# Booked arrivals of q and k stacks, row maxima on GpSimd's DMA queue, and a reordered start of the output projection in an attention and GLU kernel

## The chip, the cores and the metric

The kernel runs on one core of a Trainium2 chip. The metric is the device time of one execution in microseconds. Engines are named as in the profile: PE is TensorE, DVE is VectorE, ACT is ScalarE, POOL is GpSimd, SP is SyncE, which here issues nearly all DMAs.

## The reference

```
x: (1, 2048, 576)   wqkv: (576, 1728)   wo: (576, 576)
w_gate, w_up: (576, 4608)   w_down: (4608, 576)          all float32

xn = layernorm(x)
q, k, v = split(xn @ wqkv) into 32 heads of 18 columns
p  = softmax(q k^T / sqrt(18))           # 2048 x 2048 per head
s  = (p v) @ wo
b  = ((xn @ w_gate) * (xn @ w_up)) @ w_down
out = x + s * silu(b)
```

## The kernel before, in words

**Number format.** Products are made of float32r parts: a value is split into a high part (an ACT copy that rounds) and a low part (a subtraction on DVE or POOL), and high x high, high x low and low x high are summed. For q and k the parts lie above each other in the partitions: a *stack* has three times 18 rows. `ring` and `pair0`, `pair1` are tiles of 128 partitions; rows 0 to 53 serve the a items of a head, rows 64 to 119 the b items. `load_pair(r, h)` fetches a whole stack (three DMAs, 0.44 MB), `load_ring(r, h, k)` half of one (three DMAs, 0.22 MB), both from the scratch `sqk` in HBM by SP's queue.

**Stages.** First layernorm, q, k and v; then the main loop (`order`), which holds attention and the GLU at once; then the output projection (line 1156 to the end), which multiplies by `wo`, applies silu and adds x.

**Attention in the main loop.** A head has 64 *a items* and 64 *b items*. An a item (`a_item`) is a product q k^T of 128 queries by 512 keys and DVE's maximum of each row. After the last a item of a head, `max_fold` and `max_rows` fold the maxima, split them, transpose them into the tile `mt`, and write them with four DMAs of 4 KB as two more rows (R and R + 1) of the q stack that the b items use; the last head writes them to both row halves. A *b item* (`b_item`) is a product k q^T with these rows in it, and ACT's exponential into a `pt` tile. A *visit* multiplies up to seven blocks of four pt tiles by v (`pv_group`, L625); where it ends a head, `finish` divides on DVE and stores the result to `sot` with four DMAs on SP.

**The GLU in the main loop.** The work is cut in 72 units: 4 chunks c of 512 rows of x by 18 slices q of the hidden width. Two *streams* use the two halves of PE's rows (0 to 63 and 64 to 127) side by side: stream 0 makes the up products, stream 1 the gate products (L658, 27 for each of a unit's two parts n), and both make the down products of the unit before (L700). `gate_end` multiplies gate and up on DVE, splits on ACT and POOL (hs, L674) and fetches the next weights `wgu`; `turn_round` copies hs across the two halves as `hx`. At the end of a chunk the next x columns come in 18 loads (`x_block`).

**The planner.** The order of all these instructions is decided while the program is written, by a loop in `order` that keeps a clock for each stream (`clk`), for DVE, ACT and POOL (`free`), and one for the DMA engines (`queue`). `moved(start, size)` books a transfer: the queue moves on by size / 0.24 (MB and us) and the transfer counts as there 2.0 us later. `can_go` holds a stream's next product until the booked wgu, hx, wd or x is there. If a stream is held, an a or b item may be taken in its place. Items otherwise go by goals (`a_goal`, `b_goal`): b items follow `N + LEAD` = 88 places behind a items, and `b_ready` asks for the maxima to be there (`rows_done`, DVE's end plus 6.0 us).

Wanted stacks wait in the list `stacks`. They are sent at gate ends, up to two at a time, and this is booked; those left over are sent by `feed` at items 20, 48 and 52 of a head, and this is not booked. No a or b item asks when its stack arrives.

```
f(*a)
moved(fin + 1.4, 0.44 if f is load_pair else 0.22)      # at a gate end
...
want[0](*want[1])                                        # in feed
```

The loads of `wo` (`wo_load`, 1.47 MB) are not booked either, nor SP's wait at `finish`.

**The start of the projection.** After the last visit, `prefetch` puts `high` (ACT, L805) and `low` (DVE, L810) of the first three row blocks of the attention result, columns 0 to 511, in the list `later`; `small` takes from it while the last down products are planned. Behind the loop come five `w_split` (wo's high parts on ACT, L817, low parts on POOL, L818), and then `chores_done` empties the list.

Engines run their own instructions in program order. SP and POOL issue DMAs in that order too, and an issue that waits holds those behind it.

Of the kernel before, what the change touches and what calls it, by code (L numbers as in the profile page):

```python
# [40 lines left out]
def kernel(  # L41
# [98 lines left out]
    def chores_done():  # L140
        while chores or later:
            chore()
# [421 lines left out]
    with ExitStack() as mid:  # L564
# [27 lines left out]
        def max_rows(h):  # L592
            m = ms.pop(h)
            mm = mp.tile([128, 2, NT], FR, name="mm", bufs=1)
            mt = mp.tile([128, 32], FT, name="mt", bufs=1)
            nc.vector.tensor_scalar(mm[:, 0, :], m, -1.0, None, op0=OP.mult)
            nc.vector.scalar_tensor_tensor(mm[:, 1, :], m, -1.0, mm[:, 0, :].bitcast(FT),
                                           op0=OP.mult, op1=OP.subtract)
            nc.vector.transpose(mt, mm.rearrange("p a t -> p (a t)").bitcast(FT))
            for r in (64, 0) if h == H - 1 else (64,):  # L600
                q = ring if r == 0 else pairs[h % 2]
                for g in range(4):
                    rows = q[r + R:r + R + 2, :].rearrange("j (t g i) -> j g t i", g=4, i=32)[:, g].bitcast(FT)
                    nc.sync.dma_start(rows, mt[32 * g:32 * g + 32, :])

        pt, PARTS = {}, 29

# [172 lines left out]
        def prefetch(now):  # L780
            mid.close()
            ep = fin["ep"] = ctx.enter_context(tc.tile_pool(name="end", bufs=1, reuse_waits="tile"))
            loads.extend((fetch, (t,), 0.59) for t in range(4))
            quiet[0] = max(clk) + 2.0
            for k in range(3):
                later.extend([(high, (k, 0)), (low, (k, 0))])

        def begin():
            lo.extend(stk.tile([128, S], FR, name=f"o{k}", tag=tag) for k, tag in enumerate(("pair0", "pair1", "ring")))
# [41 lines left out]
        def stream(r):  # L831

            for u in range(len(units) + 1):
                for n in (2 * u, 2 * u + 1):
                    if u == len(units):
                        break
                    c, q = units[u]
                    box = []
                    for k in range(len(TERMS)):
                        def work(n=n, k=k, box=box, c=c, q=q):  # L840
                            if k == 0:
                                box.append(gu_start(r, n))
                            gu_op(r, n, box[0], k)
                            if q == NF2 - 1 and n % 2 and k % 3 == 2 and c < NCH - 1:
                                x_block(c + 1, k // 3, (64 * r,))
                                there["x", c + 1, k // 3, r] = moved(clk[r] + 0.5, 0.262)
                            if k == len(TERMS) - 1:
                                (gate_end if r else up_end)(n, box[0])
                                if r and n == 2 * len(units) - 1:
                                    wo_load()  # L850
                        end = (("DVE", 0.60) if r else ("ACT", 0.50)) if k == len(TERMS) - 1 else None
                        yield LONG, k == 0, work, end, ("g", n, k)
                for s in range(4):
                    if not u:
                        break
                    box = []
                    for k in range(len(DTERMS)):
                        def work(s=s, k=k, box=box, u=u - 1):
                            if k == 0:
                                box.append(down_start(r, u))  # L860
                            down_op(r, u, s, box[0], k)
                            if k == len(DTERMS) - 1:
                                down_end(r, u, s, box[0])
                        end = ("DVE", 0.365) if k == len(DTERMS) - 1 else None
                        yield SHORT, k == 0, work, end, ("d", u - 1, 12 * s + k)
# [16 lines left out]
        def next_free(tag):  # L882
            if tag == "g":
                return min(banks["g"])
            return banks[tag][turn[tag] % len(banks[tag])]

        def engine(eng, start, taken):
            free[eng] = max(free[eng], start) + taken
            return free[eng] + TAIL[eng]
# [26 lines left out]
            return a_goal(i) if i < TOTAL else a_goal(TOTAL) + LAST * (i - TOTAL)  # L916


        def feed(r, h, i):

            if i == 0:
                if h:
                    stacks.append((load_ring, (r, h, 1)))
                if h + 1 < H and (r or h):
                    stacks.append((load_pair, (r, h + 1)))
            if i == 32 and h + 1 < H:
                stacks.append((load_ring, (r, h + 1, 0)))
            for at, want in ((20, (load_ring, (r, h, 1))), (48, (load_pair, (r, h + 1))), (52, (load_ring, (r, h + 1, 0)))):
                if i == at and want in stacks:
                    stacks.remove(want)  # L930
                    want[0](*want[1])

        def a_next(r=0):
            nonlocal na
# [11 lines left out]

        def b_ready(r=1):
            h = nb // N
            return nb < TOTAL and rows_done.get(h, 1e9) <= clk[r] and len(due) * 4 + nb % 4 + 1 <= PARTS

        def b_next(r=1):
            nonlocal nb
# [46 lines left out]
        def visit(now):  # L999

            now = max(now, *clk)
            many = 0
            now += 0.095
            if due:
                now = max(now, next_free("g") - EARLY + 0.03)
            for h, t, at in due:
                if at > now + 0.5 * many + 0.3 or many == size(due[0]):
                    break
                now += 0.859
                many += 1  # L1010
            now -= 0.859 * many
            for h in sorted({h for h, _, _ in due[:many]}):
                ts = [t for g, t, _ in due[:many] if g == h]
                now = max(now, next_free("g") - EARLY + 0.03) + 0.859 * len(ts)
                k = banks["g"].index(next_free("g"))
                pv_group(h, ts, k)
                end = engine("DVE", now + 0.25, 0.60) if ts[0] else engine("ACT", max(now + 0.25, shown[0]), 0.495)
                banks["g"][k] = end + EARLY
                if ts[-1] == NT - 1:
                    finish(h)  # L1020
                    engine("DVE", end, 0.60)
                    engine("DVE", 0.0, 0.85)
                    shown[0] = engine("DVE", 0.0, 0.60)
            del due[:many]
            clk[0] = clk[1] = issued[0] = now + 0.13
            fresh[:] = True, True
# [40 lines left out]
        def order():  # L1067
# [5 lines left out]
            while any(heads) or na < TOTAL or nb < TOTAL or due:  # L1073
# [18 lines left out]
                lean = PULL * (gone[0] - gone[1] - SKEW) * (1 if r else -1)  # L1092

                if r == 0 and (na < TOTAL or nb < TOTAL - N) or r == 1 and nb == 0 and na < N:
                    at, goal, score, can = next_free("a"), a_goal(na) + lean, a_next, na < TOTAL and na < nb + N + MOST
                    can = can and not late(goal, r)
                else:
                    at, goal, score, can = next_free("b"), b_goal(nb) + lean, b_next, b_ready(r)
# [9 lines left out]
                elif op is not None:  # L1108
# [8 lines left out]
                    if end:  # L1117
# [9 lines left out]
                        elif r == 0:  # L1127
                            upped[n] = done
                        else:
                            gated[n] = done  # L1130
                            fin = engine("ACT", done + 0.05, 0.535)
                            fin = engine("POOL", fin + 0.05, 1.29)
                            loaded[n] = moved(done - 0.4, 1.18) if (n // 2 + 1) % NF2 else 0.0
                            if n // 2 == len(units) - 1:
                                there["h", n // 2] = moved(fin, 0.524)
                            elif n == 1:
                                there["h", 0] = moved(fin, 1.05)
                            for _ in range(2):
                                hot = n + 2 >= 2 * NF2 and n % (2 * NF2) in (34, 35, 0) and n + 2 < 2 * len(units)
                                for want in stacks:  # L1140
                                    if hot and (want[0] is load_pair or n % (2 * NF2) == 2 * NF2 - 1):
                                        continue
                                    stacks.remove(want)
                                    f, a = want
                                    f(*a)
                                    moved(fin + 1.4, 0.44 if f is load_pair else 0.22)
                                    break
                    heads[r] = next(feeds[r], None)
                else:
# [11 lines left out]
        f(*a)  # L1161
    for k in range(5):
        w_split(k)
    chores_done()
    for t in range(12, NT):
        def end_silu(e, t=t):
# [100 lines left out]
```

## Time and profile before

| | us |
|---|---|
| median of 3 runs | 2609.0 |
| the runs, lowest to highest | 2608.26 to 2611.98 |
| the profiled execution | 2607.05 |
| its span, first to last instruction | 2605.2 |

The profile is that of the one execution in the third row; its span starts at 0, and all places below are us from there. Its mean granted PE clock is 0.999. The main loop's products run from about 199 to 2536 us and the products with wo from there to 2599 us. Rows of the profile name an engine, the line of the kernel, what is written and read (`out<-in`), and counts; "PE pb L614 <- DMA ring<-sqk" in a list of waits means that PE's instruction on line 614, which writes pb, waited for the DMA that fills ring.

### The profile page before, as it was taken

How to read it: one execution, taken by the hardware profiler on the slowest of the kernel's cores; microseconds unless marked ns; L12 is line 12 of the kernel's file. 1: busy time of each engine (PE TensorE's matmuls, PEld its weight loads, DVE VectorE, ACT ScalarE, POOL GpSimd, SP SyncE). 2: the span in 40 equal slices, each digit the busy share in tenths (PEclk: the TensorE clock that was granted, in tenths of full speed). 3: DMA queues.
4: the chain of work that ended last, by engine and by line, in shares of the span. 5: the costliest groups of instructions: out<-in, count | busy, mean ns of one | idle time of the engine just before them, and what ended most of it. 6: DMA issues, size and time to landing. Idle time of an engine off the chain costs nothing.

```text
span 2605.2 us, 59028 instructions
## 1 busy us (share of the span) xinstructions
PE 2577.5 (99%) x24360; PEld 2109.0 (81%) x24360; DVE 1923.8 (74%) x3373; ACT 1463.7 (56%) x2698; POOL 447.9 (17%) x402
## 2 busy tenths in 40 slices
PE   8999999999999999999999999999999999999998
PEld 6899877777878888887888878877878888877878
DVE  6208777777868888877788788777788888777537
ACT  5222666666655555655555565655555665555561
POOL 3114433333311111000001101000000110100016
PEclk9999999999999999999999999999999999999999
DMA  7799988888885566566676556655585666655557
GB/s 239 222 285 267 268 224 228 227 212 227 218 203 165 175 177 179 171 175 169 177 182 188 165 172 180 178 163 174 156 203 157 174 188 172 178 173 166 150 162 254
DMA packets 195077, 504.44 MB, mean 194 GB/s; under 512 B 56888, under 2 KB 114872, under 8 KB 155768
## 3 DMA queue, kind: packets, MB, share of 16 engines
q1 hardware_dynamic: 192648, 492.70, 67.6%
q0 software_dynamic: 2160, 7.96, 0.8%
q8 instruction: 192, 3.15, 0.6%
q14 instruction: 77, 0.63, 0.1%
HBM read 312.21 MB, written 107.61 MB: 161 GB/s over the span
## 4 chain that ended last, share of the span: by engine, by line
PE 94%; DMA 2%; DVE 2%; POOL 1%; ACT 0%; issue 0%; SPq 0%; POOLq 0%; DVEq 0%; ACTq 0%
PE pg L658 34%; PE pg L625 17%; PE pg L700 16%; PE pa L582 11%; PE pb L614 9%; PE pg L392 2%; PE pa L338 2%; PE pb L338 2%; POOL ys L1211 1%; DMA hx<-hs 0%; DMA xc<-sx 0%; DMA ring<-sqk 0%; DMA o<-sot 0%; DMA gin<-sg 0%; DMA wgu<-swg 0%
## 5 line engine op out<-in xcount | busy, mean ns | idle before, releaser
L584 DVE TENSOR_REDUCE mx<-pa 128x1 f32<-128x512 f32 x2048 | 1364.0, 686 | 161.1 <-PE pa L582 77.9
L616 ACT ACTIVATE pt<-pb 128x512 f32<-128x512 f32 x2048 | 1155.7, 597 | 568.7 <-PE pb L614 484.7
L658 PE MATMUL pg<-xc,wgu 64*128 64x512 f32 x7776 | 1396.7, 392 | 0.6 <-DMA wgu<-swg 0.6
L658 PEld LDWEIGHTS pg<-xc,wgu 64*128 64x128 f32 x7776 | 1056.6, 186 | 47.9 <-DVE acc L728 1.1
L614 PE MATMUL pb<-pair,ring 56*128 56x512 f32 x2006 | 789.1, 399 | 3.3 <-DMA ring<-sqk 3.3
L582 PE MATMUL pa<-pair,ring 54*128 54x512 f32 x2001 | 785.0, 398 | 0.7 <-DVE mx L584 0.7
L700 PE MATMUL pg<-wd,hs 64*128 64x288 f32 x3408 | 536.4, 292 | 1.2 <-DVE acc L728 1.2
L700 PE MATMUL pg<-wd,hx 64*128 64x288 f32 x3408 | 528.7, 292 | 2.0 <-DMA hx<-hs 2.0
L674 POOL TENSOR_TENSOR hs<-us,hs 128x512 fp32r<-128x512 f32 x144 | 186.3, 1294 | 1775.6 <-ACT hs L673 1682.4
L700 PEld LDWEIGHTS pg<-wd,hs 64*128 64x128 f32 x3408 | 473.6, 186 | 6.0 <-DVE acc L728 1.9
L700 PEld LDWEIGHTS pg<-wd,hx 64*128 64x128 f32 x3408 | 467.3, 185 | 5.7 <-DMA hx<-hs 2.6
L625 PE MATMUL pg<-pt,vt 128*32 128x512 f32 x4096 | 456.5, 596 | 0.0
L582 PEld LDWEIGHTS pa<-pair,ring 54*128 54x128 f32 x2001 | 363.1, 184 | 84.8 <-issue 48.6
L614 PEld LDWEIGHTS pb<-pair,ring 56*128 56x128 f32 x2006 | 364.7, 184 | 15.5 <-issue 4.6
L625 PEld LDWEIGHTS pg<-pt,vt 128*32 128x32 f32 x4096 | 125.9, 110 | 285.6 <-issue 281.9
L631 DVE TENSOR_TENSOR oc<-oc,pg 128x512 f32<-128x512 f32 x69 | 47.5, 688 | 323.9 <-PE pg L625 317.5
L728 DVE TENSOR_TENSOR acc<-acc,pg 128x288 f32<-128x288 f32 x544 | 235.1, 446 | 26.8 <-PE pg L700 24.2
L673 ACT ACTIVATE hs<-us 128x512 fp32r<-128x512 f32 x144 | 91.2, 634 | 155.0 <-DVE us L670 153.6
L191 POOL TENSOR_TENSOR wgu<-wraw,wgu 128x384 fp32r<-128x384 f32 x108 | 108.6, 1017 | 106.2 <-ACT wgu L190 91.9
L629 ACT ACTIVATE oc<-pg 128x512 f32<-128x512 f32 x32 | 19.2, 600 | 189.3 <-PE pg L625 166.2
L670 DVE TENSOR_TENSOR us<-pg,us 128x512 f32<-128x512 f32 x144 | 98.3, 683 | 17.9 <-PE pg L658 14.8
L663 ACT ACTIVATE us<-pg 128x512 f32<-128x512 f32 x144 | 86.1, 598 | 28.2 <-PE pg L658 24.9
(125 smaller groups left out, 1206.9 us busy)
## 6 DMA issues: line engine op xcount, KB each, us to landing
wgu<-swg SPq DMA_DIRECT2D x102, 1152.0 KB
hx<-hs SPq DMA_DIRECT2D x142, 512.0 KB
wd<-swd SPq DMA_DIRECT2D x50, 1152.0 KB
swg<-wgu SPq DMA_DIRECT2D x36, 1152.0 KB
pair<-sqk SPq DMA_DIRECT2D x192, 144.0 KB
ring<-sqk SPq DMA_DIRECT2D x384, 72.0 KB
swd<-wd SPq DMA_DIRECT2D x18, 1152.0 KB
sqk<-hl SPq DMA_DIRECT2D x32, 512.0 KB
```

Source lines behind the costliest of these rows:

```text
L191: nc.gpsimd.tensor_tensor(w[:, 9 + b:12 + b, :], raw[:, b:b + 3, :], w[:, b:b + 3, :].bitcast(FT), op=OP.subtract)
L338: nc.tensor.matmul(p, wq[b, a], xcs[c][:, e, :], start=n == 0, stop=n == len(PAIRS) - 1)
L582: nc.tensor.matmul(p, q[rows, t * 128:(t + 1) * 128], k[rows, c * 512:(c + 1) * 512], start=True, stop=True)
L584: nc.vector.tensor_reduce(mx[h][:, t, c:c + 1], p, axis=AX.X, op=OP.max)
L614: nc.tensor.matmul(p, k[rows, t * 128:(t + 1) * 128], q[rows, c * 512:(c + 1) * 512], start=True, stop=True)
L616: nc.scalar.activation(pt[t, c], p, AF.Exp, scale=scale)
L625: nc.tensor.matmul(p[32 * c:32 * c + 32, :], vt[h // 2][:, t, 6 * (h % 2):6 * (h % 2) + 32], pt[t, c], start=t == ts[0], stop=t == ts[-1])
L658: nc.tensor.matmul(ps, gw[n][half[r], a, :], xg[i][half[r], e, :], start=k == 0, stop=k == len(TERMS) - 1)
L670: nc.vector.tensor_tensor(h32, ps, h32, op=OP.mult)
L674: nc.gpsimd.tensor_tensor(hj[:, 1, :], h32, hj[:, 0, :].bitcast(FT), op=OP.subtract)
L700: nc.tensor.matmul(ps[:, 0:HALF], (hx if k else hs)[u][half[r], j, a, s * 128:(s + 1) * 128], dw[u][half[r], k, j, e, :], start=n == 0, st ...
L728: nc.vector.tensor_tensor(a, a, ps[:, 0:HALF], op=OP.add)
```

## The change

Three things change.

1. Every stack that is sent, by a gate end or by `feed`, is booked and its arrival noted (`send`, `arrives`). `stacked(r, n)` is true when the stacks of item n are noted as there, or nothing is noted for them; a and b items are taken only then. `wo_load` and SP's wait at a finish (`shown`) are booked too.
2. The DMAs of the maxima's rows are issued by POOL in place of SP.
3. `high` and `low` of the first three row blocks leave the list `later`. Each `high` stands behind one of the first three `w_split`, the three `low` behind all five.

```
                 for g in range(4):
                     rows = q[r + R:r + R + 2, :].rearrange(...)
-                    nc.sync.dma_start(rows, mt[32 * g:32 * g + 32, :])
+                    nc.gpsimd.dma_start(rows, mt[32 * g:32 * g + 32, :])
...
             loads.extend((fetch, (t,), 0.59) for t in range(4))
-            quiet[0] = max(clk) + 2.0
-            for k in range(3):
-                later.extend([(high, (k, 0)), (low, (k, 0))])
...
                                     wo_load()
+                                    moved(max(clk), 1.47)
...
+        arrives = {}
+
+        def send(want, now):
+            f, a = want
+            f(*a)
+            arrives[f.__name__, *a] = moved(now, 0.44 if f is load_pair else 0.22)
+
+        def stacked(r, n):
+            h, i = divmod(n, N)
+            keys = [("load_ring", r, h, i // 32)] + [("load_pair", r, h)] * (i == 0)
+            return all(arrives.get(k, 0.0) <= max(clk) for k in keys)
...
                     stacks.remove(want)
-                    want[0](*want[1])
+                    send(want, max(clk))
...
-            return nb < TOTAL and rows_done.get(h, 1e9) <= clk[r] and ...
+            return nb < TOTAL and stacked(64, nb) and rows_done.get(h, 1e9) <= clk[r] and ...
...
                     shown[0] = engine("DVE", 0.0, 0.60)
+                    queue[0] = max(queue[0], shown[0])
...
-  ... a_next, na < TOTAL and na < nb + N + MOST
+  ... a_next, na < TOTAL and na < nb + N + MOST and stacked(0, na)
...
                                     stacks.remove(want)
-                                    f, a = want
-                                    f(*a)
-                                    moved(fin + 1.4, 0.44 if f is load_pair else 0.22)
+                                    send(want, fin + 1.4)
...
     for k in range(5):
         w_split(k)
+        if k < 3:
+            high(k, 0)
+    for k in range(3):
+        low(k, 0)
     chores_done()
```

More of the change, by code (lines that the diff above doesn't have):

```diff
@@ L948, in b_ready @@
             h = nb // N
-            return nb < TOTAL and rows_done.get(h, 1e9) <= clk[r] and len(due) * 4 + nb % 4 + 1 <= PARTS
+            return nb < TOTAL and stacked(64, nb) and rows_done.get(h, 1e9) <= clk[r] and len(due) * 4 + nb % 4 + 1 <= PARTS
         def b_next(r=1):
@@ L1094, in order @@
                 if r == 0 and (na < TOTAL or nb < TOTAL - N) or r == 1 and nb == 0 and na < N:
-                    at, goal, score, can = next_free("a"), a_goal(na) + lean, a_next, na < TOTAL and na < nb + N + MOST
+                    at, goal, score, can = next_free("a"), a_goal(na) + lean, a_next, na < TOTAL and na < nb + N + MOST and stacked(0, na)
                     can = can and not late(goal, r)
```

## The prediction, made before the change was run

> **What bounds the kernel now.** I read the page's busy times and its chain first, then the stretches (busy time of each engine by window), then the list of waits of TensorE (PE).
>
> ```profile
> PE 2577.5 (99%) x24360; PEld 2109.0 (81%) x24360; DVE 1923.8 (74%) x3373; ACT 1463.7 (56%) x2698; POOL 447.9 (17%) x402
> PE 94%; DMA 2%; DVE 2%; POOL 1%; ACT 0%; issue 0%; SPq 0%; POOLq 0%; DVEq 0%; ACTq 0%
> ```
>
> PE is busy for 2577.5 of 2605.2 us and carries 94% of the chain. Nothing here can be won by making another engine faster; only places where PE stands still, or runs at half clock, can give time back. The stretches say where these are (columns: window, busy us and instructions of PE, PEld, DVE, ACT, POOL, granted clock, DMA share, GB/s).
>
> ```profile
> 700.00:730.00 30.00, 30.00 (x300) 24.82 (x298) 24.51 (x43) 20.17 (x38) 8.85 (x9) 1.00 0.69 200
> ...
> 750.00:768.00 18.00, 15.72 (x139) 15.26 (x135) 15.02 (x25) 12.78 (x23) 4.16 (x3) 1.00 1.03 255
> ```
>
> An ordinary stretch has no idle PE at all. The stretch 750:768 has 18 - 15.72 = 2.3 us of it, with the DMA engines full (1.03). It lies where the second quarter of the rows, c = 1, begins: 18 loads of x, then stacks of q and k, share the DMA engines. All waits of PE that the trace knows are few (columns: total us, times, longest):
>
> ```profile
> PE pb L614 <- DMA ring<-sqk: 3.3, 1, 3.3
> PE pg L700 <- DVE acc L728: 2.2, 3, 1.0
> PE pg L700 <- DMA hx<-hs: 2.0, 1, 2.0
> PE pa L1197 <- POOL wos L818: 1.1, 1, 1.1
> ...
> PE pg L658 <- DMA wgu<-swg: 0.6, 1, 0.6
> ...
> PE pa L1197 <- ACT hi L805: 0.5, 1, 0.5
> ```
>
> So the change can win single waits of 0.5 to 3.3 us, and it can lose as much as a worse order of work costs. The largest is a stack: the first b item of head 7 waits for its half of ring. The chain shows how it came about (start us, us, what).
>
> ```profile
> 750.34 8.20 DMA xc<-sx
> 758.55 1.65 SPq L239
> 760.24 1.56 SPq L239
> 761.85 7.12 DMA ring<-sqk
> ```
>
> Its load was issued from 758.55 on, behind the x loads, and landed at 761.85 + 7.12 = 768.97, and the planner had put the b item ahead of a visit (56 products with v) that was ready.
>
> **Part 1: stacks count in the order.** The change has the planner book every stack's transfer and refuse an a or b item whose stack is, by that booking, not there. At head 7 the visit, and products of the two streams, then come first and the 3.3 us are filled. The wait costs more than itself:
>
> ```profile
> 769.45 7.91 PE L625 MATMUL pg<-pt,vt 128*32 128x512 f32 x56
> 302.81 6.22 PE L625 MATMUL pg<-pt,vt 128*32 128x512 f32 x56
> 769.00:773.00 4.00, 3.95 (x22) 1.18 (x26) 0.00 (x0) 0.60 (x1) 0.00 (x0) 0.62 0.35 108
> 280.00:284.00 4.00, 3.82 (x47) 3.64 (x49) 2.75 (x5) 2.03 (x4) 0.72 (x1) 1.00 0.94 319
> ```
>
> The same 56 products take 6.22 us elsewhere and 7.91 us right behind the wait, because the granted clock falls to 0.62 in that stretch. That is 7.91 - 6.22 = 1.7 us more. Together -5.0 us (3.3 + 1.7); the bounds are 0 (the wait only moves) and -5.0. After the shorter wait of 2.0 us, at 280, the clock stayed at 1.00. The Trainium skill ("TensorE: Matmul & The Clock Gate", Part 1) says that the clock halves after an idle window of about 3.4 us and that the window runs free; by that rule a wait cut only in half would already save the 1.7 us, and both waits here agree with it.
>
> What the refusal costs: where the booking is later than the true landing, a filler is refused, or a stream is held, for nothing. The booking also grows: stacks sent from feed (0.22 or 0.44 MB at 0.24 MB per us, so 0.9 or 1.8 us each by the planner's own figures) now push the booked arrivals of wgu, wd, hx and x behind them, and so does a visit that finishes a head, through shown. For the second there is a reason in the trace (waits of SP's queue):
>
> ```profile
> SPq L645 <- DVE oc L642: 196.5, 29, 13.4
> ```
>
> SP does stand for 196.5 / 29 = 6.8 us at a finish with its later loads behind it. But in the whole run PE waited for hx only once, 2.0 us, so a hold on account of a later booking is mostly pure loss: one of the two row halves of the array goes empty. Where a stream is held the planner takes an a or b item as a filler, and the two streams balance later, so a hold of x us costs at most x and perhaps half of it. Bounds: 0, and 71 down groups times 1.8 us = 128 us if a whole stack stood ahead of each hx and none were absorbed. I take +1 us, near the lower end, because the stretch row of 700:730 (30.00 of 30) shows streams without any hold and most arrivals lie well ahead of their use. This is my weakest number.
>
> **Part 2: rows of maxima through GpSimd's queue.** 132 DMAs of 4 KB leave SP and go to POOL. On SP they stood ahead of other loads:
>
> ```profile
> 254.04 4.55 SPq L604 DMA_DIRECT2D pair<-mt  x4
> ...
> 268.51 3.19 SPq L690 DMA_DIRECT2D hx<-hs  x2
> 2443.73 4.02 SPq L604 DMA_DIRECT2D pair<-mt  x4
> 2447.80 5.10 SPq L604 DMA_DIRECT2D ring<-mt  x4
> 2453.00 3.63 SPq L182 DMA_DIRECT2D wgu<-swg  x2
> ```
>
> In the last head the eight of them hold SP from 2443.73 to 2453.00, and the loads of wgu behind them make PE wait 0.6 us; free of them these go out some 9 us earlier, so -0.6 us (bounds 0 and -0.6). At 254 they take 4.55 us of SP ahead of the hx whose lateness makes the 2.0 us wait. SP is packed from there to 268.51, so hx can go out up to 4.55 us earlier, but the store and loads between have waits of their own and the DMA engines are almost full there. I take half, -1.0 us; bounds 0 and -2.0.
>
> On POOL they add 132 issues. The nearest rows are its present DMAs and what a head's rows meet there:
>
> ```profile
> L1213 POOL DMA_DIRECT2D out_dram<-ys x15 | 8.5, 565 | 4.5 <-POOL ys L1211 3.6 <-DMA xi<-in_A_x_dram 0.3 <-DMA o<-sot 0.3
> sg<-sil POOLq DMA_DIRECT2D x12, 288.0 KB, 7.3
> 249.69 0.21 DVE L599 STREAM_TRANSPOSE mt<-mm 128x32 f32<-128x32 f32 x1
> 251.82 1.30 POOL L674 TENSOR_TENSOR hs<-us,hs 128x512 fp32r<-128x512 f32 x1 [5.75 <-ACT hs L673]
> 262.21 0.40 PE L614 MATMUL pb<-pair,ring 56*128 56x512 f32 x1
> ```
>
> At 565 ns and 4.5/15 = 0.3 us of idle each, four cost 3.5 us, 114 us in all on an engine that is busy for 447.9 of 2605.2. POOL now stands at the head of a head's rows until DVE's mt is there; behind it in order are hs (L674), the splits of weights and silu's last step. In the first head POOL is free at 249.9, issues until 253.4, and hs slips from 251.82 by 1.6 us; the hx that needs it went out at 268.51, so nothing on the path. The rows land at the latest 3.5 + 7.3 = 10.8 us after mt, that is at 260.7, and the first b item reads them at 262.21. The first head has the least room, since the planner puts b items LEAD = 24 items behind in all others. Cost 0; if the cover went, 1 to 2 us once. Bounds 0 and +3.
>
> **Part 3: w_split, high and low.** ACT stands in the end at the first high and the splits of wo queue behind it:
>
> ```profile
> 2532.99 0.63 ACT L805 ACTIVATE hi<-o 128x512 fp32r<-128x512 f32 x1 [7.39 <-DVE tp L641]
> 2534.27 8.29 POOL L818 TENSOR_TENSOR wos<-wor,wos 128x576 fp32r<-128x576 f32 x5 [15.35 <-ACT wos L817]
> 2551.21 0.63 ACT L805 ACTIVATE hi<-o 128x512 fp32r<-128x512 f32 x1 [3.42 <-DMA o<-sot]
> 2554.29 1.03 PE L1197 MATMUL pa<-wos,hi 128*128 128x288 f32 x6 [0.44 <-DVE ys L1206]
> ```
>
> Afterwards the first split is ahead of it and can go some us earlier, so POOL's next four end up to 8.29/5 = 1.7 us earlier and the 1.1 + 0.5 us of PE's waits go. What is late next: PE resumes at 2554.29 only when DVE has got past the low that needs o, which lands at 2551.2 and later, and SP issues it in the same order behind the last head's result. PE would come to that place 1.6 us earlier and wait 1.6 us longer. The three lows behind the last down sums are covered by the first 48 products. So 0; bounds -1.6 and +1.
>
> **Sum.** -5.0 - 1.0 - 0.6 + 1 + 0 + 0 = -5.6 us against the profiled execution's 2607.05 us (span 2605.2), which lies 1.95 us under the median of 2609.0. On the median's scale 2609.0 - 5.6 = 2603.4 us.
>
> **The rivals.**
> 1. *The wait only moves.* At 750:768 the DMA engines are full (1.03); if x is what both streams lack, refusing the b item leaves PE idle in its place, and clock and time are lost as before. Against it: a visit of 6.2 us was ready right behind it. The loss comes back, the +1 stays, 0.6 to 1.6 are won: 2608 to 2609.
> 2. *Slower: the heavier booking holds the streams.* Place: the start of each down group, held for hx. Price: a hold of x us in each of 71 groups, half of it lost. It decides from 0.31 us a group on: 71 x 0.31 / 2 = 11 us eat the 5.6 and 5.2 more. One stack of 1.8 us in two groups of five gives 71 x 0.4 x 1.8 / 2 = 26 us, less the 6.6 won: 2628. For it: SP's 196.5 us at L645 and the stacks sent from feed, which were not booked; against it: PE's full stretches and the fillers.
> 3. *DVE holds POOL's issues.* The trace shows DVE steps that grow long where POOL works:
>
> ```profile
> L749 DVE TENSOR_SCALAR sil<-sil 128x576 f32<-128x576 f32 x12 | 5.4, 451 | 0.0
> L749 DVE TENSOR_SCALAR gl<-gl 128x576 f32<-128x576 f32 x4 | 4.9, 1216 | 0.0
> ```
>
> The same step takes 451 ns in the loop and 1216 ns in the end, where POOL is at work. If each of four issues lost 0.8 us, rows would land 3.1 us later and only the first head's b items would wait, 3.1 - 1.5 = 1.6 us: 2605. The Trainium skill ("SBUF — State Buffer", "SBUF: two separate sides") speaks against the move: GpSimd cannot write its descriptors while DVE runs an operation that takes the shared ports, and SP's queue is free of that. No row of before shows it on a DMA.
>
> **How the numbers follow.** About 0.2% (5.2 us) is what a measurement here can tell from no change, so faster means under 2603.8. The forecast, with both long waits filled, stands barely on that side; better fillings at the two other quarters and fewer blocked loads on SP can add to it. Forecast 0.58, of which a tenth falls short of 5.2 us (0.05); rival 1 0.20; rival 3 0.07; rival 2 0.15. Faster 0.58 - 0.05 = 0.53; same 0.05 + 0.20 + 0.07 = 0.32; slower 0.15. The range leaves out 0.1 on either side: down to 2595 (all bounds won, 2609 - 5.0 - 2.0 - 0.6 - 1.6 = 2599.8, and 5 us of gains through the order that no row prices), up to 2613 (the beginning of rival 2).
>
> **What would show it.** Right: no wait of PE for ring, an L625 group near 6.2 us at head 7, clock 1.00 until the end, no wait for wgu in the last head, 132 issues on POOL of 0.6 to 0.9 us, the w_splits ahead of the first high, a wait of about 2 us for ys at the fifth tile. Wrong: windows in the loop with PE under 30.00 of 30, waits of PE for pair<-mt, a new wait for x at 750, or an end that is shorter from 2530 on by over 1 us.

## The result, and the profile after

The changed kernel takes 2605.9 us (median of 20 runs, 2600.72 to 2608.95); the kernel before took 2609.55 us in its 20 runs beside it. The medians lie 3.7 us apart; the ratio is 0.9984 (95% interval 0.9977 to 0.9991), 0.16% faster. The forecast was 2603.4 us, 5.6 us faster.

The page's busy times and chain of after:

```profile
span 2604.5 us, 59060 instructions
PE 2579.5 (99%) x24360; PEld 2115.4 (81%) x24360; DVE 1920.7 (74%) x3373; ACT 1462.6 (56%) x2698; POOL 526.3 (20%) x534
PE 96%; DMA 2%; DVE 1%; issue 1%; ACT 1%; POOL 0%; SPq 0%; POOLq 0%; ACTq 0%; DVEq 0%
```

POOL has 132 instructions and 78 us more, as it should with the rows' DMAs. PE's waits in after (total us, times, longest) are the first surprise:

```profile
PE pb L614 <- DMA ring<-sqk: 3.9, 1, 3.9
PE pa L1210 <- ACT hi L802: 2.1, 2, 1.4
PE pg L700 <- DMA hx<-hs: 1.2, 1, 1.2
PE pg L700 <- DVE acc L728: 1.2, 2, 0.7
...
PE pa L582 <- DVE mx L584: 0.3, 1, 0.3
PE pa L1210 <- POOL wos L815: 0.2, 1, 0.2
```

The wait for ring, which the booking of stacks was to fill, is still there and no shorter: 3.9 us against 3.3. The wait for wgu in the last head has gone. At the start of the projection the wait for wos has shrunk from 1.1 to 0.2 us, but that for hi has grown from 0.5 to 2.1 us (line 805 of before is 802 now). The stretches (busy us and instructions of PE, PEld, DVE, ACT, POOL, granted clock, DMA share, GB/s) show what the two waits drag behind them:

```profile
762.00:769.00 7.00, 3.14 (x28) 2.48 (x28) 2.08 (x3) 2.42 (x5) 0.06 (x1) 1.00 0.92 303
769.00:773.00 4.00, 4.00 (x24) 0.98 (x20) 0.00 (x0) 0.49 (x1) 0.00 (x0) 0.57 0.26 72
2537.00:2541.00 4.00, 3.63 (x15) 3.29 (x16) 2.03 (x2) 2.03 (x5) 4.00 (x3) 0.57 0.91 256
```

The clock is at 0.57 after the ring wait, as before the change, and now once more at 2537, in the first products with wo.

The reason is in the program, not in the chip. Set against the kernel before, PE's instructions stand in the same order down to the last visit; only there do the last down products go behind the visit instead of around it. A kernel before with only the booking and the refusal of stacks (`send`, `arrives`, `stacked`) has the same instructions in the same order on every engine. By the planner's clock every stack, that of head 7 too, was there in time, so the rule never once refused an item.

### The profile page after: what moved, and what is told of

It is laid out like the page before. It is cut to its first block, busy times and chain, and to the rows that moved or that the text cites. A ratio compares the mean times of both kernels' runs of the same rounds, so it can differ in the third digit from the quotient of the medians.

```text
span 2604.5 us, 59060 instructions
## 1 busy us (share of the span) xinstructions
PE 2579.5 (99%) x24360; PEld 2115.4 (81%) x24360; DVE 1920.7 (74%) x3373; ACT 1462.6 (56%) x2698; POOL 526.3 (20%) x534
## 4 chain that ended last, share of the span: by engine, by line
PE 96%; DMA 2%; DVE 1%; issue 1%; ACT 1%; POOL 0%; SPq 0%; POOLq 0%; ACTq 0%; DVEq 0%
PE pg L658 34%; PE pg L625 17%; PE pg L700 15%; PE pa L582 11%; PE pb L614 9%; PE pg L392 2%; PE pa L338 2%; PE pb L338 2%; PE pg L1210 1%; PE pa L1210 1%; PE pb L1210 1%; DMA ring<-sqk 0%; DMA hx<-hs 0%; ACT xn L286 0%; DMA xc<-sx 0%
## 5 line engine op out<-in xcount | busy, mean ns | idle before, releaser
L625 PE MATMUL pg<-pt,vt 128*32 128x512 f32 x4096 | 456.5, 596 | 0.0
L625 PEld LDWEIGHTS pg<-pt,vt 128*32 128x32 f32 x4096 | 125.9, 110 | 285.6 <-issue 282.0
L604 POOL DMA_DIRECT2D pair<-mt x128 | 76.6, 604 | 225.1 <-DVE mt L599 223.8
```

The costliest lines, as they stand in the source:

```text
L625: nc.tensor.matmul(p[32 * c:32 * c + 32, :], vt[h // 2][:, t, 6 * (h % 2):6 * (h % 2) + 32], pt[t, c], start=t == ts[0], stop=t == ts[-1])
```

## The experiments

Every run below was timed in five rounds beside the kernel before.

**Rows alone.** Edit to the kernel before:

```
-                    nc.sync.dma_start(rows, mt[32 * g:32 * g + 32, :])
+                    nc.gpsimd.dma_start(rows, mt[32 * g:32 * g + 32, :])
```

> The kernel before with only the maxima's rows on POOL's queue. Theory A (most of the 3.6 us comes from the loads that the rows held up on SP): 2 to 3 us faster than before, ratio 0.9989 to 0.9992, no wait of PE for wgu in the last head, the wait for hx near 280 about 1.2 us in place of 2.0. Theory B (the gain comes from the end, where the booked load of wo changes the order): within 0.5 us of before, and the waits for hx and wgu stand as they were.

Measured: 2606.09 us against 2609.58 us beside it, ratio 0.9989 (0.9981 to 0.9998). By the ratios this single line gives 0.11% (2.9 us) of the 0.16%, by the medians 3.5 of the 3.7 us. The wait for wgu is gone from its list, but the wait for hx near 280 is 2.1 us: that part of theory A failed.

**Rows back on SP**, the same line undone in the changed kernel.

> The changed kernel with the maxima's rows back on SP. Theory A (all of the gain comes from the rows): the gain is gone, ratio to the kernel before 0.9998 to 1.0008, and the waits for wgu and for hx near 280 are back at 1 to 2 us. Theory B (booking and the new end carry part): ratio 0.9988 to 0.9995.

Measured: 2609.5 us, ratio 0.9999 (0.9990 to 1.0008); the waits for wgu and hx are 1.1 and 1.7 us. Without the rows on POOL no gain is left that the run shows, though its interval allows 0.1%. That the rows carry the gain stands from both sides; that the hx near 280 has a share in it does not.

Where the rows gave time can be read from the traces, because PE's order is the same. In the last head SP's queue, of after:

```profile
2447.93 8.19 SPq L182 DMA_DIRECT2D wgu<-swg  x2
```

The first of the two loads of wgu starts 5.1 us earlier than in before (2453.00; the second, at 2455.80, only 0.5 us) and nobody waits; the rows' eight issues, 9.1 us of SP, are no longer ahead of them. The other place was not foreseen. DVE and POOL at the end of head 4, before and then after:

```profile
535.67 0.92 DVE L596 TENSOR_SCALAR mm<-m 128x16 fp32r<-128x16 f32 x1
535.55 1.02 POOL L191 TENSOR_TENSOR wgu<-wraw,wgu 128x384 fp32r<-128x384 f32 x1
```

```profile
535.42 0.18 DVE L596 TENSOR_SCALAR mm<-m 128x16 fp32r<-128x16 f32 x1
536.35 2.38 POOL L604 DMA_DIRECT2D pair<-mt  x4 [1.14 <-DVE mt L599]
538.75 2.96 POOL L191 TENSOR_TENSOR wgu<-wraw,wgu 128x384 fp32r<-128x384 f32 x3
```

Before, the split of weights on POOL started 0.12 us ahead of DVE's mm and mm took 0.92 us; it ended with POOL's instruction. After, POOL stands at the rows, waiting for mt, and cannot start the split in that moment: mm takes 0.18 us. Over 32 heads the groups by line say the same, before and after:

```profile
L596 DVE TENSOR_SCALAR mm<-m 128x16 fp32r<-128x16 f32 x32 | 9.0, 282 | 1.1
L596 DVE TENSOR_SCALAR mm<-m 128x16 fp32r<-128x16 f32 x32 | 7.5, 235 | 1.1
```

1.5 us less in all. It is the same in every kernel with this order up to the last visit: with the rows on SP (before and three runs) mm is long at heads 4, 5 and 6 (0.9, 0.7 and 0.4 us), with them on POOL (after and two runs) at none of these. Each long mm began while POOL was in an instruction and ended 0.02 to 0.03 us after it. So at these heads the wait that the change adds on POOL keeps POOL out of DVE's way. This hangs on the order: in the runs with a margin below, which have the rows on POOL too, mm takes 9.4 us in all.

At head 4 PE's wait for mx goes (0.7 to 0.3 us in the lists of waits). Set product by product against before, PE comes 0.6 to 0.7 us ahead at head 4, 0.3 to 0.4 us at head 5 and 0.9 to 1.0 us at the last head's wgu in each of the three traces with the rows on POOL, and at none of these places in the three others with them on SP. These places make 1.9 us. The rest of the 2.9 us lies inside its interval; also, before's profile has a small wait for wgu: it is 0.6 us there, and 1.1 to 1.6 us in the other three with the rows on SP.

**The booking of wo alone.** Edit to the kernel before:

```
                                     wo_load()
+                                    moved(max(clk), 1.47)
```

> The kernel before with one line more, the booking of wo's load; the only order that it changes is that of the last visit, which moves ahead of the last down products, and of the loads behind it. Theory A: within 1 us of before; the products with wo start about 2 us earlier, and two stacks of o come behind the last head's result, so PE waits some 2 us for high parts and may lose 1.7 us to a halved clock. Theory B: 2.5 to 4 us faster, ratio 0.9985 to 0.9990.

Measured: 2611.9 us, ratio 1.0007 (0.9999 to 1.0016): no gain, and a loss is not shown. The products with wo do not start 2 us earlier but later (2539.30 us against 2536.22): PE waits for wos ahead of the first. Its waits in the end:

```profile
PE pa L1198 <- ACT wos L817: 2.3, 2, 2.1
PE pa L1198 <- ACT hi L805: 1.8, 1, 1.8
```

The booked load holds the last down products, so the last visit goes first, and it holds the loads of o: only one of three goes out ahead of the last head's result, at which SP stands.

**high and low alone**, part 3 of the change put into the kernel before.

```
     for k in range(5):
         w_split(k)
+        if k < 3:
+            high(k, 0)
+    for k in range(3):
+        low(k, 0)
```

> The kernel before with high and low of the first three row blocks moved as in the change, nothing else. Prediction's step 3: PE's waits for wos and hi at the start of the projection (1.1 and 0.5 us) shrink, the wait for ys at the fifth tile grows by as much, time within 0.5 us of before. Rival: the 1.6 us come through to the end, ratio 0.9994.

Measured: ratio 1.0003 (0.9995 to 1.0012). The waits for wos and hi are gone from its list, and at the fifth tile stands, in PE's timeline:

```profile
2557.94 1.19 PE L1198 MATMUL pa<-wos,hi 128*128 128x288 f32 x6 [2.78 <-DVE ys L1207]
```

0.4 us before, 2.8 us now: what was won in front (waits of 1.1 and 0.5 us) is waited for at the last o block, as the prediction had it.

**Early loads of o in the changed kernel.**

```
-            loads.extend((fetch_o, (k, c), 0.262) for c in range(2) for k in range(3))
+            for k in range(3):
+                fetch_o(k, 0)
+                moved(max(clk), 0.262)
+            loads.extend((fetch_o, (k, 1), 0.262) for k in range(3))
```

> The changed kernel, but the first columns of o's first three row blocks are loaded at once when the last b item is placed, ahead of the last head's result on SP; the order of PE is the same. If these loads, late behind that result, are what makes PE wait some 2 us for high parts and halves its clock at 2537: those waits gone, clock 1.00 there, then a wait for ys at the fifth tile, and 1 to 1.5 us won over the changed kernel (ratio to before 0.9978 to 0.9981). If the fifth tile's wait takes all back: within 0.5 us of the changed kernel.

Measured: 2604.28 us, ratio 0.9982 (0.9974 to 0.9991), which the run cannot tell from the changed kernel's 0.9984. The wait for ACT's hi has gone and the clock stays up there, and the fifth tile gets the wait:

```profile
2551.54 1.03 PE L1213 MATMUL pa<-wos,hi 128*128 128x288 f32 x6 [2.69 <-DVE ys L1222]
```

**A margin on the stacks.** In the changed kernel a stack counts only 3.0 us after its booking:

```
-            return all(arrives.get(k, 0.0) <= max(clk) for k in keys)
+            return all(arrives.get(k, -9.0) + 3.0 <= max(clk) for k in keys)
```

> The changed kernel, but a stack counts as there only 3.0 us after its booked arrival; in the order nothing differs ahead of the first b item of head 7, which now stands behind the visit. If the booking is right in kind and only too early (the forecast's mechanism): no wait for ring of 3 us or more near 766, clock 1.00 at 770, and about 5 us faster than the changed kernel (2600 to 2602; ratio to before 0.996 to 0.997). If the wait only moves (rival 1 of the prediction): another wait of 2 to 4 us and a halved clock between 750 and 790, time within 1.5 us of the changed kernel. If the stricter rule holds streams elsewhere: the ring wait gone and the time 2605 or more, with stretches behind 790 under 30.00 of 30.

Measured: 2604.56 us, ratio 0.9981 (0.9971 to 0.9990): the forecast of 2600 to 2602 us was missed, and the run cannot tell its time from the changed kernel's 0.9984. Yet no wait for ring is left in its list. Head 7's visit and the stretches:

```profile
762.00:769.00 7.00, 7.00 (x64) 3.53 (x65) 2.58 (x4) 2.49 (x5) 0.57 (x1) 1.00 0.89 277
769.00:773.00 4.00, 4.00 (x42) 2.13 (x36) 1.46 (x3) 1.09 (x2) 0.00 (x0) 1.00 0.08 16
765.13 6.22 PE L625 MATMUL pg<-pt,vt 128*32 128x512 f32 x56
```

PE is busy for 7.00 of 7 us where it was 3.14, the visit takes 6.22 us and not 7.91, the clock stays at 1.00. Counted from its first a product, the first a product of head 9 comes at 619.4 us against 624.5 in after: 5.1 us, as the forecast had it for this place. Yet the last product with wd comes only 0.7 us earlier (2333.8 against 2334.5 on that scale). The planner's order from head 7 on is another. At the last a item 5.2 us are still won (2236.4 against 2241.6), so the loss lies behind it, in the last heads. There, the margin's run and then after:

```profile
2490.00:2520.00 30.00, 30.00 (x252) 22.65 (x248) 4.85 (x9) 18.94 (x35) 2.58 (x2) 1.00 0.48 133
2490.00:2520.00 30.00, 30.00 (x288) 20.70 (x286) 5.23 (x10) 17.57 (x34) 2.59 (x2) 1.00 0.51 142
```

PE is "busy" for 30.00 us in both, but with 252 against 288 instructions. Most of the difference is the short products of visits, 60 against 88 (the same windows for L625 alone; busy us and instructions of PE and PEld, clock, DMA share, GB/s):

```profile
2490.00:2520.00 30.00, 6.45 (x60) 1.61 (x56) 1.00 0.48 133
2490.00:2520.00 30.00, 9.86 (x88) 2.65 (x88) 1.00 0.51 142
```

The others tell more: the 192 products of the streams and b items take the other 23.6 us, where after fits 200 in 20.1 us. From 2491.88 to 2495.22 us, for one, products go to one half of the array only. A busy share does not show that; counts by line do. How much of the loss it makes was not measured.

**Margin and early loads together.**

> Stacks counted as there 3.0 us after their booked arrival, and the early loads of o, together. If the two gains are of different places and add: 2.5 to 3 us under the changed kernel, ratio to before 0.9972 to 0.9977. If the end is bound by the last o blocks (k = 3, 4 of the second columns) whatever comes ahead: as with the margin alone, 0.998.

Measured: 2602.35 us (8 runs), ratio 0.9972 (0.9961 to 0.9983), the lowest ratio of all, though its interval meets that of the margin alone. Its wait at the fifth tile is 0.8 us. That the two gains add is not shown more closely than the intervals allow.

**Margin and rows, with the old end.** The kernel before with the rows on POOL, stacks booked with the margin, and nothing of the rest.

> The kernel before with the rows on POOL and the stack rule with a margin of 3.0 us; wo and SP's wait at a finish are not booked and high and low stand as before. The run with the margin alone won 5 us at head 7 to 16 and lost some 3 us in its end. If the new end loses them: 2 to 3 us under that run, 2601.5 to 2603, ratio 0.9970 to 0.9976. If the end's time does not depend on these: within 1 us of it, ratio 0.998.

Measured: 2605.51 us, ratio 0.9983 (0.9975 to 0.9992). The run gives no sign that the new end is what gave the 3 us back; with the old end they are gone as well. Here too the time goes behind the last a item: that comes 6.8 us earlier than in after, the last product with wd 2.3 us later.

**A heavier booking.** In the changed kernel:

```
-            return queue[0] + 2.0
+            return queue[0] + 4.0
```

> The changed kernel with every transfer booked as there 4.0 us after the queue instead of 2.0: wgu, hx, wd, x and stacks alike. This prices rival 2 of the prediction (a heavier booking holds the streams at their down products). If that rival's price is right (2 us more at each of 71 down groups, half of it lost): up to 71 us slower, and at least 15, ratio to before over 1.004. If fillers and the balance of the streams take the holds up: between 3 us faster and 5 us slower than the changed kernel, and since stacks count later too, the wait for ring near 766 may be gone.

Measured: 2625.33 us, ratio 1.0058 (1.0044 to 1.0072), 19 us slower than the changed kernel. The slower rival's mechanism exists, but its place was misjudged. Stretches of this run and of after:

```profile
900.00:1300.00 400.00, 398.77 (x3918) 321.88 (x3914) 319.40 (x553) 233.20 (x420) 49.05 (x50) 1.00 0.61 172
900.00:1300.00 400.00, 400.00 (x3936) 326.17 (x3932) 317.47 (x554) 234.14 (x421) 48.36 (x49) 1.00 0.63 175
```

In this stretch of the loop 2 us more on every transfer cost 18 of 3936 instructions, 0.5%; from 1500 to 1800 us they cost none (2951 against 2946). The wait for ring is gone, as expected. The last a item comes 4.2 us later than in after, on the scale above. The last product with wd comes 23.7 us later: most is lost behind the last a item, where a items are no longer there as fillers. PE waits for hxl there (3.1 us, and a clock of 0.57 from 2547 to 2555); the rest was not placed. In the first head PE also waits 4.0 us for the rows from POOL (pair<-mt), the place where the prediction saw the least room.

## Why the prediction was right, and where it was not

The direction and the range held (2605.9 in 2595 to 2613), and the time falls in the case "within 0.2%", to which I gave 0.32. That the sum came near is luck: -5.0 of its -5.6 us belong to a step that did nothing, and the measured gain comes from the rows, to which I had given -1.6.

- *Part 1, -5.0 and +1: both were 0.* The step that failed is that the planner, by its booking, would refuse the b item of head 7. I read from the trace that the stack landed late (768.97 us) and took it that the planner's own booking would say so. The booking had it there 2.9 us behind its queue (0.22 / 0.24 + 2.0), where the chain of before shows 7.12 us for it, with the DMA engines full: the b item passed. The rest of the step was right, and the margin's run shows it: the visit was ready, it fills the wait, and wait and clock together are worth 5.1 us there. The cost of +1 could not arise either, since no order changed before the last visit.
- *Part 2, -0.6 and -1.0.* The mechanism at wgu holds and the wait of 0.6 us is gone (its first load goes out 5.1 us earlier, where I had taken some 9). For hx, 1.2 us after, 2.1 and 1.5 us in two other kernels with the rows on POOL, and 1.7 us with them back on SP: no gain shown. SP was packed there, and hx went out no earlier: at 269.24 in after, against 268.51. The mm that POOL no longer holds up at heads 4 to 6 was missed. POOL's costs were right: 604 ns an issue where I took 565, 5.0 us to landing where I allowed 7.3, and PE nowhere in after waits for rows.

```profile
L604 POOL DMA_DIRECT2D pair<-mt x128 | 76.6, 604 | 225.1 <-DVE mt L599 223.8
pair<-mt POOLq DMA_DIRECT2D x128, 4.0 KB, 5.0
```

  POOL stands for 223.8 us at the rows, and no wait of PE comes from it.
- *Part 3, 0.* Right for high and low, shown by the run with them alone. What I left out is that booking wo moves the last visit and the loads of o. The first product with wo comes 2.0 us earlier (2534.23 against 2536.22), of which some 1.4 us were won ahead of the last visit; then the wait for hi and the halved clock take back most of it. The wait for ys at the fifth tile, which I had named as a sign, is not in after's list.
- *Rivals.* Rival 1 has the outcome at the ring wait (it stays), though not the reason: nothing was refused. Rival 2 did not occur; forced by the heavier booking, it costs less per down group than I priced (1 us of every 2 us would be 71 us; 19 us were lost in all), and most of it behind the last a item. Rival 3, that DVE holds POOL's issues up, is not seen: issues of 604 ns beside the 565 ns of before. The Trainium skill ("SBUF — State Buffer", "SBUF: two separate sides") says that the ports which DVE and GpSimd share are locked by whichever of the two starts first; the mm rows agree with it, at heads 4 to 6 in the direction that speaks for the move.

## What to carry to other kernels

A rule in a planner works only through the numbers that it compares: before a new condition is priced, ask whether it is ever false, and compare the instruction order of the two programs. Where TensorE sets the time, count its instructions by line in a stretch beside its busy time, for an array with one half empty is also busy. An edit that gives back one wait in a chain of loads is worth what the next late load allows: at the fifth tile nothing that a run could tell, twice. And a gain can come from a place that nobody aimed at, here DVE's mm.

## What the runs showed of the hardware that I had not expected

The same wait costs differently from run to run. After 3.2 to 3.3 us of waiting for ring, the visit of 56 products took 6.22 us in one profiled execution, 7.91 in the kernel before, 8.78 and 8.99 in two others. The visits of the run with the rows back on SP, and of the run with high and low moved:

```profile
770.81 6.22 PE L625 MATMUL pg<-pt,vt 128*32 128x512 f32 x56
771.23 8.99 PE L625 MATMUL pg<-pt,vt 128*32 128x512 f32 x56
```

and their granted clock there (column behind POOL; same runs, same order):

```profile
766.00:778.00 12.00, 8.75 (x80) 3.53 (x78) 2.23 (x4) 2.21 (x4) 0.00 (x0) 1.00 0.48 155
766.00:778.00 12.00, 8.82 (x54) 2.96 (x54) 1.38 (x2) 1.80 (x4) 0.00 (x0) 0.72 0.48 143
```

Behind this wait the clock halves for no, one or two stretches of 3.41 us (one from 769.96 us in before, two from 769.05 to 775.88 us with the rows alone). Shorter waits can do it too. With the rows back on SP, PE waits 1.7 us for hx near 280 and the clock halves; before's wait of 2.0 us in that place left it at 1.00:

```profile
277.43:280.84 3.41, 1.72 (x19) 1.35 (x17) 0.98 (x2) 1.22 (x4) 0.00 (x0) 1.00 0.98 269
280.84:284.25 3.41, 3.41 (x30) 3.41 (x28) 2.34 (x4) 1.70 (x4) 1.25 (x1) 0.50 0.90 326
```

So it does not hold that a wait cut only in half would already save the 1.7 us of clock, as the prediction had it. That the cost varies fits the Trainium skill ("TensorE: Matmul & The Clock Gate", Part 1), whose window runs free of the kernel; but its rule that the clock halves after an idle window does not fit, since PE was busy for 1.72 us of the 3.41 us ahead of the halved clock here. A wait of 3 us was worth 3 to 6 us, and part of the spread between runs (2600.72 to 2608.95 us of one program) may come from it; that part was not measured.
